# Wider MoE units: three units of 512 tokens in place of four of 384, in a gated-linear-attention and MoE kernel

## The chip, the core and the metric

The kernel runs as one program on one core of a Trainium2 chip. The engines named below are TensorE (PE, with its weight loads PEld), VectorE (DVE), ScalarE (ACT), GpSimd (POOL) and the engine that issues most DMAs (SP). The time of a run is the device time in microseconds (us); of several runs the median counts. A profile is one execution, recorded instruction by instruction; its span goes from the first to the last instruction.

## What is computed

The inputs are q, k, v and gate logits f for 4 sequences, 8 heads, 768 tokens and 48 features a head. The first half is a gated linear recurrence, whose output (4 sequences of 768 tokens, 8 x 48 = 384 features) is the input x of the second:

```
f = 1/(1+exp(-f_logit))
state = f[t] * state + outer(k[t], v[t]);   y[t] = q[t] @ state          # each head, t = 0..767
h = max(x @ w_in, 0)                                                     # 384 -> 1024 features
conv_out[t] = conv_w[0]*h[t-1] + conv_w[1]*h[t] + conv_w[2]*h[t+1]       # zero outside a sequence
out = (h * sigmoid(conv_out)) @ w_out                                    # 1024 -> 384
```

## The kernel before

**Chunks.** Attention works on chunks of 128 tokens: 24 chunks in all, 6 in a sequence. For each chunk n the order knows steps with a letter: F, L, M, V load f, k, q and v; x and p take exponentials and logarithms on ACT; G sums the logits; K and Q scale k and q (`scaled_q`, line 324: on POOL from chunk 5 on); k transposes k on PE (`ptk`, line 330); a computes the scores (`pa`, lines 345 and 351) and masks them on DVE; s adds to the state (`pk` on PE, lines 371 and 376, an addition on DVE, a product on POOL, line 386); y computes the output (`py`, line 398) in two halves, from the masked scores and from the state and the scaled q. The chunk's output goes, as a rounded part and a remainder, into the tile xT of its MoE unit.

**MoE units.** The 3072 tokens are cut into eight units of 384 tokens, two to a sequence. Unit u has for each of eight groups f of 128 features a step `m{u}.{f}` (`hidden`): nine matmuls into one PSUM tile `ph` (three slices of the 384 inputs, each as high x high, high x low and low x high part, line 454), the ReLU on ACT into h_b (line 457), the middle tap of the convolution on ACT (line 462) and the outer taps on DVE (lines 464 and 466). For each pair of groups there are `h{u}.{fp}` (`carried`: the last two columns of the unit before, or zeros, into h_b, ACT, line 435) and `j{u}.{fp}` (`gated`: tanh on ACT, line 473, and the product with h on DVE, line 475).

**Results.** `r{b}.{m}` (`result`) makes the output of one chunk: the gated values are split into a rounded part gh (ACT, line 493) and a remainder gl (DVE, line 495), 24 matmuls of 384 columns go into a PSUM tile `po` (line 507), ACT copies it out (line 512) and a DMA writes it. The tokens of one result can lie in two units, since a unit's last token waits for its right neighbour.

**Buffers.** The gated values of a unit are one tile of eight groups x 385 columns, of which there are two; the raw weights are staged in the same two buffers at the start. ph, po and some attention tiles share three PSUM buffers.

**The order.** Nothing is scheduled by the compiler. Every step is a generator; the table ORDER is a list of step names, and each mention runs its step on to its next `yield`. So the table alone sets the order in which the instructions of all steps stand on each engine; each engine works in that order and waits where an operand or a buffer is not ready. PE gets matmuls of several ph, po and attention steps in turn.

Of the kernel before, what the change touches and what calls it, by code (L numbers as in the profile page):

```python
# [9 lines left out]
F32 = mybir.dt.float32  # L10
# [7 lines left out]
P = 128  # L18
# [11 lines left out]
x5 V2 M3 K3 x4 y1 H1.0 J0.1 k2 a2 k2 a2 h0.2 x5 I1.1 O3 s1 y1 s1 F6 p3 J2.1 s1 J2.1 J2.1 H2.0 y1 Q3 J0.1 G4 J2.1 J1.1 G5  # L30
L5 H2.0 M5 s2 s2 y2 L6 p4 J0.1 p4 y2 J0.1 y2 J1.1 y2 Q4 J0.1 a3 h0.0 O0 x6 k3 J1.1 J1.1 V3 h0.6 m0.1 x6 F11 P3 H0.1 F8
s2 P3 H2.1 m0.3 m0.3 k3 t3 P3 K4 a3 J1.1 G6 m0.3 t4 m0.1 m0.1 y3 m0.1 P3 J1.1 y3 P3 m0.3 P0 p5 h0.4 s3 a4 y3 V6 P3 P0 p5
x8 s3 x8 V4 O5 K5 H0.1 F9 m0.0 O2 a4 m0.0 k4 m0.2 m0.0 P5 Q5 P5 m0.1 k4 m0.2 M6 m0.7 S3 m0.0 m0.1 H1.1 P0 P0 p6 p6 y3 P0
s3 S3 m0.4 F10 H2.1 m0.2 m0.0 a5 s4 y4 x9 m0.2 y4 P0 P2 H1.1 O4 P2 Q6 y4 G8 O6 a5 L8 m0.7 m0.5 M8 P5 m0.2 P5 s4 m0.7 t6
m0.7 L7 x9 s4 m0.1 V5 O1 m0.4 K6 y4 m0.3 m0.2 P5 m0.5 m0.4 m0.0 P2 t5 m0.6 m0.3 m0.0 P2 p7 m0.4 m0.5 V7 m0.6 K7 k6 m0.6
m0.5 m0.2 y5 m0.3 P5 y5 k6 p7 t7 y5 p8 m0.5 a6 k7 y5 m1.1 m0.6 a6 m1.0 M7 G9 M9 m0.4 S0 m1.3 m0.5 j0.0 m0.4 k7 m1.1 m1.1
P1 j0.2 S5 P2 m1.0 m1.0 p8 S0 F12 Q7 j0.0 a7 h1.0 L9 m1.1 s6 K8 S5 L10 s6 m0.7 Q8 m1.0 a7 y6 k8 P1 P1 m1.2 m0.5 m0.7
m1.3 k8 j0.2 P1 V9 m1.5 m0.6 h1.2 m1.2 m1.2 m0.4 p9 m1.5 m1.3 s7 P2 K9 P4 s7 P1 P4 j0.4 a8 y6 y6 m1.2 P4 P4 S2 m1.3 P1
F13 k9 p9 y7 k9 y7 m1.2 V8 m0.6 m1.4 j0.4 s7 m1.5 a8 m1.7 y7 m1.4 y7 m1.3 m1.4 F14 y8 m1.1 V11 m0.6 m0.7 y8 S1 x12 m1.3
a9 M10 t8 h1.4 L11 m1.5 S2 m1.2 Q9 P4 m1.4 G10 P4 O7 m1.5 P6 P6 a9 s8 j0.6 m1.4 j0.6 y8 S4 y8 h1.6 P6 m1.7 P7 m1.7 m1.2  # L40
s8 P7 m1.6 s8 m1.7 m1.6 M12 m1.6 m1.3 m2.3 p10 m2.3 p10 m2.2 a9 m2.3 m1.6 r0.0 m2.5 m2.2 m1.4 j1.2 L12 K10 r0.1 j1.2
m2.5 m2.2 P6 P6 S1 m2.5 k10 y9 k10 m2.3 m1.5 Q10 S4 a10 s9 m1.7 y9 M13 a10 m2.4 P6 h2.2 P7 P7 S6 m2.2 P7 m2.4 M11 r0.0
t9 r0.0 m1.5 m1.4 S6 j1.4 P7 j1.4 S7 m2.4 S7 m2.5 r0.0 r0.1 m1.1 m1.0 r0.0 y9 r0.0 r0.0 m1.6 r0.1 G11 m1.1 p11 m1.6 r0.1
# [684 lines left out]
```

## Time and profile before

| what | us |
|---|---|
| median of 3 runs | 305.09 |
| lowest and highest of them | 304.69, 307.47 |
| time of the profiled execution | 305.0 |
| its span | 303.3 |
| busy: PE / DVE / ACT / POOL | 294.2 / 251.3 / 220.5 / 85.3 |

The profiled execution took 0.1 us less than the median; 1.7 us of its time lie outside its span. Busy time of PE counts each matmul to its modelled end, and matmuls overlap: the next starts before the last has ended. So what one matmul costs is read from the distance of starts, not from its length.

### The profile page before, as it was taken

What the parts mean: (1) busy time and instruction counts of PE and PEld (TensorE: products, weight loads), DVE (VectorE), ACT (ScalarE), POOL (GpSimd) and SP (SyncE); (2) the same over time, 40 slices, a digit from 0 to 9 for tenths busy, and PEclk for the clock granted to TensorE, in tenths of its full rate; (3) what the DMA queues carried; (4) which work ended last, traced back from release to release, by engine and by line L of the source; (5) the groups of instructions that cost most, each with busy time, mean ns of one, the idle gap of its engine ahead of it and who ended that gap; (6) DMA issues with size and microseconds to landing.
All of it is one profiled execution on the core that took longest, in us unless ns stands there. A gap on an engine that the chain in (4) does not pass through costs nothing.

```text
span 303.3 us, 8894 instructions
## 1 busy us (share of the span) xinstructions
PE 294.2 (97%) x3747; PEld 273.5 (90%) x3747; DVE 251.3 (83%) x380; ACT 220.5 (73%) x422; POOL 85.3 (28%) x107
## 2 busy tenths in 40 slices
PE   7799989999999999999999999999999999999994
PEld 5678878988999999999998999999999999999994
DVE  4999999999999999977999999946893976479520
ACT  4999979989967996767976995665756544676521
POOL 5475894344503140300323410230305010000000
PEclk9999999999999999999999999999999999999999
DMA  7999951194025411627315130602012000000211
GB/s 230 396 385 391 403 191 39 56 333 135 2 72 161 101 59 61 220 72 224 102 37 166 64 124 2 195 2 84 3 30 89 2 28 26 28 1 2 79 54 55
DMA packets 19374, 35.67 MB, mean 118 GB/s; under 512 B 2156, under 2 KB 9092, under 8 KB 19332
## 3 DMA queue, kind: packets, MB, share of 16 engines
q1 hardware_dynamic: 19044, 34.69, 33.8%
q8 instruction: 30, 0.49, 0.7%
q10 hardware_dynamic: 288, 0.39, 0.4%
q14 instruction: 12, 0.10, 0.1%
HBM read 30.35 MB, written 4.72 MB: 116 GB/s over the span
## 4 chain that ended last, share of the span: by engine, by line
PE 75%; DVE 7%; POOL 3%; issue 1%; ACT 1%; POOLq 0%
PE po L507 31%; PE ph L454 28%; PE py L398 8%; PE pa L351 3%; PE ptk L330 2%; DVE g L466 2%; PE pk L376 2%; DVE g L464 2%; DVE g L475 1%; POOL st L386 1%; PE pa L345 1%; DVE am L358 1%; PE pk L371 1%; POOL q L324 1%; DVE gl L495 1%
## 5 line engine op out<-in xcount | busy, mean ns | idle before, releaser
L454 PE MATMUL ph<-xT,wih 128*128 128x384 f32 x384 | 99.6, 340 | 0.0
L454 PEld LDWEIGHTS ph<-xT,wih 128*128 128x128 f32 x384 | 68.3, 188 | 1.0 <-issue 0.2
L507 PE MATMUL po<-woh,gh 128*128 128x384 f32 x192 | 64.7, 337 | 0.0
L454 PE MATMUL ph<-xT,wil 128*128 128x384 f32 x192 | 64.3, 335 | 0.0
L507 PE MATMUL po<-wol,gh 128*128 128x384 f32 x192 | 64.2, 334 | 0.0
L507 PE MATMUL po<-woh,gl 128*128 128x384 f32 x192 | 64.2, 334 | 0.0
L464 DVE SCALAR_TENSOR_TENSOR g<-hb,cw,g 128x384 f32<-128x384 f32 (+1 forms) x64 | 42.2, 667 | 13.0 <-ACT g L462 12.9
L466 DVE SCALAR_TENSOR_TENSOR g<-hb,cw,g 128x384 f32<-128x384 f32 (+1 forms) x64 | 40.5, 649 | 0.7
L457 ACT ACTIVATE hb<-ph 128x384 f32<-128x384 f32 x64 | 30.7, 487 | 11.4 <-PE ph L454 10.8
L495 DVE TENSOR_TENSOR gl<-g,gh 128x1024 fp32r<-128x1024 f32 (+4 forms) x34 | 30.4, 908 | 9.6 <-ACT gh L493 9.6
L462 ACT ACTIVATE g<-hb,cw 128x384 f32<-128x384 f32 (+1 forms) x64 | 38.0, 614 | 0.3
L507 PEld LDWEIGHTS po<-woh,gh 128*128 128x128 f32 x192 | 36.0, 188 | 0.5 <-issue 0.2
L324 POOL TENSOR_TENSOR q<-q,fd 128x512 f32<-128x512 f32 x19 | 26.9, 1419 | 33.0 <-ACT fd L307 24.3
L507 PEld LDWEIGHTS po<-wol,gh 128*128 128x128 f32 x192 | 36.0, 188 | 0.0
L507 PEld LDWEIGHTS po<-woh,gl 128*128 128x128 f32 x192 | 36.0, 188 | 0.0
L454 PEld LDWEIGHTS ph<-xT,wil 128*128 128x128 f32 x192 | 36.0, 188 | 0.0
L493 ACT CAST gh<-g 128x1024 fp32r<-128x1024 f32 (+4 forms) x34 | 26.4, 800 | 12.7 <-PE po L507 8.8
L386 POOL TENSOR_TENSOR st<-st,ft_all 128x256 f32<-128x256 f32 x16 | 20.8, 1301 | 51.7 <-DVE st L384 51.7
L475 DVE SCALAR_TENSOR_TENSOR g<-g,hb 128x768 f32<-128x768 f32 (+1 forms) x32 | 30.1, 952 | 3.7 <-ACT g L473 3.7
L512 ACT COPY ob<-po 128x384 f32<-128x384 f32 x24 | 11.3, 474 | 29.7 <-PE po L507 27.1
L473 ACT ACTIVATE g<-g 128x768 f32<-128x768 f32 (+1 forms) x32 | 26.7, 846 | 3.9 <-DVE g L466 3.8
L312 POOL COPY ft_all<-fd 128x4 f32<-128x4 f32 x24 | 12.7, 537 | 56.5 <-ACT fd L307 56.5
(92 smaller groups left out, 453.9 us busy)
## 6 DMA issues: line engine op xcount, KB each, us to landing
k<-in_k_dram SPq DMA_DIRECT2D x24, 256.0 KB, 4.4
q<-in_q_dram SPq DMA_DIRECT2D x24, 256.0 KB, 4.3
v<-in_v_dram SPq DMA_DIRECT2D x24, 224.0 KB, 4.3
fb<-in_f_logit_dram SPq DMA_DIRECT2D x18, 256.0 KB, 4.3
out_dram<-ob SPq DMA_DIRECT2D x22, 192.0 KB, 1.9
wis<-in_moe_w_in_dram SPq DMA_DIRECT2D x6, 512.0 KB, 6.0
wos<-in_moe_w_out_dram SPq DMA_DIRECT2D x8, 384.0 KB, 5.6
fb<-in_f_logit_dram SPq DMA_DIRECT2D x6, 200.0 KB, 4.9
```

Of the source, the lines that this page charges most:

```text
L324: (nc.vector if n < QV else nc.gpsimd).tensor_tensor(raw["q", n], raw["q", n], fds[n][1], ALU.mult)
L398: nc.tensor.matmul(py[G * p:G * p + G, t, :], lhs, rhs, start=start, stop=stop)
L454: nc.tensor.matmul(ph, w, xts[b, hf][:, t, xl, :], start=(k == 0), stop=(k == 3 * KT - 1))
L457: nc.scalar.activation(hb[:, 2:HS + 2], ph, AF.Relu, scale=0.5)
L462: nc.scalar.activation(cv, hb[:, 1:n + 1], AF.Copy, scale=cw[:, 1, f:f + 1])
L464: nc.vector.scalar_tensor_tensor(cv, hb[:, 2:n + 2], cw[:, 2, f:f + 1], cv, ALU.mult, ALU.add)
L466: nc.vector.scalar_tensor_tensor(cv, hb[:, 0:n], cw[:, 0, f:f + 1], cv, ALU.mult, ALU.add)
L473: nc.scalar.activation(cv, cv, AF.Tanh)
L475: nc.vector.scalar_tensor_tensor(cv, cv, 1.0, h_b[:, fp:fp + 2, 1:n + 1], ALU.add, ALU.mult)
L493: nc.scalar.copy(hi, g[:, f:f + k])
L495: nc.vector.tensor_tensor(lo, g[:, f:f + k], hi.bitcast(F32), ALU.subtract)
L507: nc.tensor.matmul(po, g[:, f, :], w, start=(i == 0), stop=(i == 3 * NF - 1))
```

## The change

Units get lengths of their own: 384, 384, 512, 512, 512, 384, 384. Units 2, 3 and 4 hold tokens 768 to 2303 (sequences 1 and 2); unit 3 holds the last 256 tokens of sequence 1 and the first 256 of sequence 2. In unit 3 the ReLU writes two halves with a gap of one column between them, and that column is set to zero by a memset on POOL; likewise the column behind a sequence's end (units 1, 4 and 6, and before in one memset at the start). This makes 16 memsets of two columns in the program's order, four for each of these units. The gated values lie in one buffer of 16 slots, one for each group of features, and group f of unit u uses slot (8u + f) mod 16; the raw weights are staged in the same buffer. A unit of 512 needs four chunks of attention before its first matmul. ORDER differs from its third line on.

```
+    UL = (384, 384, 512, 512, 512, 384, 384)
+    UB = [sum(UL[:u]) for u in range(len(UL) + 1)]
+    GS = 16
+    KF = (B - 1, NC - UL[-1] // P - 1)
-    h_b = const.tile([P, NF, HS + 4], F32, name="hb")
-    nc.gpsimd.memset(h_b[:, :, HS + 2:], 0.0)
+    h_b = const.tile([P, NF, UM + 4], F32, name="hb")
+    g_b = const.tile([P, GS, UM + 2], F32, name="gb")
...
+        def slot(u, f):
+            return (NF * u + f) % GS
         def carried(u, fp):
-            nc.scalar.copy(h_b[:, fp:fp + 2, 0:2], h_b[:, fp:fp + 2, HS:HS + 2] if u % 2 else
-                           going[:, :2, 0:1].broadcast_to([P, 2, 2]))
+            z = going[:, :2, 0:1]
+            e = 2 + width(u - 1) - last(u - 1) if u else 0
+            nc.scalar.copy(h_b[:, fp:fp + 2, 0:2], h_b[:, fp:fp + 2, e - 2:e] if UB[u] % S else z.broadcast_to([P, 2, 2]))
+            if inner(u):
+                nc.gpsimd.memset(h_b[:, fp:fp + 2, 2 + inner(u):3 + inner(u)], 0.0)
+            if last(u):
+                nc.gpsimd.memset(h_b[:, fp:fp + 2, 1 + width(u):2 + width(u)], 0.0)
             yield
         def hidden(u, f):
-            ph = ps.tile([P, HS], F32, tag="mm", name=f"ph{u}_{f}", bufs=MB)
+            L, n, s = UL[u], width(u), inner(u)
+            ph = ps.tile([P, L], F32, tag="mm", name=f"ph{u}_{f}", bufs=MB)
...
+            if s:
+                ho = hb[:, 2:2 + L + 2].rearrange("p (a c) -> p a c", a=2)[:, :, :s]
+                nc.scalar.activation(ho, ph.rearrange("p (a c) -> p a c", a=2), AF.Relu, scale=0.5)
+            else:
+                nc.scalar.activation(hb[:, 2:L + 2], ph, AF.Relu, scale=0.5)
-            cv = gts[u][:, f, :n]
+            cv = g_b[:, slot(u, f), :n]
...
 ORDER (a line of each):
-x5 V2 M3 K3 x4 y1 H1.0 J0.1 k2 a2 k2 a2 h0.2 x5 I1.1 O3 s1 y1 s1 F6 p3 J2.1 s1 J2.1 J2.1 H2.0 y1 Q3 J0.1 G4 J2.1 J1.1 G5
+x5 V2 M3 K3 x4 y1 H1.0 J0.1 k2 a2 k2 a2 h0.2 x5 I1.1 O3 s1 y1 s1 F6 p3 J2.1 s1 J2.1 J2.1 H2.0 y1 V3 G4 G5 s2 Q3 y2 F8 y2
```

What that does to the engines is seen at three places.

PE, the start of unit 2. Before, its first groups (ph_3, ph_2, ph_5) follow each other ahead of any result:

```order
L454 MATMUL ph_6_1248<-xT_1_630,wil_1_706 128x384
L454 MATMUL ph_3_1263<-xT_0_1069,wih 128x384 x2
L454 MATMUL ph_3_1263<-xT_0_1069,wil_0_271 128x384
L454 MATMUL ph_3_1263<-xT_0_1069,wih 128x384 x2
L454 MATMUL ph_3_1263<-xT_0_1069,wil_0_388 128x384
L454 MATMUL ph_2_1274<-xT_0_1069,wih 128x384 x2
```

Now the same unit starts between matmuls of the first two results, and each of its matmuls has 512 columns:

```order
L519 MATMUL po_0_1351<-woh,gl_0_1237 128x384
L465 MATMUL ph_3_1415<-xT_1056,wih 128x512 x2
L465 MATMUL ph_3_1415<-xT_1056,wil_0_269 128x512
L519 MATMUL po_1_1379<-woh,gh_1_1327 128x384
L519 MATMUL po_1_1379<-wol_1270,gh_1_1327 128x384
L519 MATMUL po_1_1379<-woh,gl_1_1328 128x384
```

The results of chunks 0 and 1 were moved ahead of unit 2, which now waits for chunk 9 in place of chunk 8. Over the whole program PE has 72 ph matmuls fewer (216 of 512 columns in place of 288 of 384) and the same po and attention matmuls.

POOL, early in the program: mswo is the staging of w_out, q_... the scaling of a chunk's q, st the product of the state. Before:

```order
L179 TENSOR_SCALAR mswo_607<-wos_409 128x384
L181 TENSOR_SCALAR mswo_607<-mswo_607 128x384
L179 TENSOR_SCALAR mswo_670<-wos_642 128x384
L324 TENSOR_TENSOR q_458<-q_458,fd_610 128x512
L181 TENSOR_SCALAR mswo_670<-mswo_670 128x384
L386 TENSOR_TENSOR st_77<-st_77,ft_all 128x256
L179 TENSOR_SCALAR mswo_762<-wos_409 128x384
L181 TENSOR_SCALAR mswo_762<-mswo_762 128x384
L324 TENSOR_TENSOR q_680<-q_680,fd_693 128x512
```

and now:

```order
L178 TENSOR_SCALAR mswo_591<-gb 128x384
L180 TENSOR_SCALAR mswo_591<-mswo_591 128x384
L310 COPY ft_all<-fd_551 128x4
L322 TENSOR_TENSOR q_499<-q_499,fd_551 128x512
L384 TENSOR_TENSOR st_77<-st_77,ft_all 128x256
L178 TENSOR_SCALAR mswo_753<-wos 128x384
L178 TENSOR_SCALAR mswo_756<-gb 128x384
L180 TENSOR_SCALAR mswo_756<-mswo_756 128x384
L180 TENSOR_SCALAR mswo_753<-mswo_753 128x384
L384 TENSOR_TENSOR st_78<-st_78,ft_all 128x256
L322 TENSOR_TENSOR q_492<-q_492,fd_666 128x512
```

The state product for chunk 4 (st_77) has one staging pair less ahead of it, and chunk 6's scaled q (q_680, now q_492) one pair and a state product more.

PE, the end of the last unit. Before, all its ph matmuls stand ahead of seven results of 24 matmuls each:

```order
L454 MATMUL ph_5_3759<-xT_1_3415,wil_1_706 128x384
L454 MATMUL ph_2_3755<-xT_1_3415,wih 128x384 x2
L454 MATMUL ph_2_3755<-xT_1_3415,wil_0_456 128x384
L507 MATMUL po_4_3798<-woh,gh_4_3623 128x384
L507 MATMUL po_4_3798<-wol_945,gh_4_3623 128x384
```

Now result 2.4 (po_4) stands in two halves between them, and six results follow the last one:

```order
L519 MATMUL po_4_3661<-wol_1392,gh_4_3544 128x384
L519 MATMUL po_4_3661<-woh,gl_4_3545 128x384
L465 MATMUL ph_5_3675<-xT_3233,wih 128x384 x2
L465 MATMUL ph_5_3675<-xT_3233,wil_1_693 128x384
L465 MATMUL ph_5_3675<-xT_3233,wih 128x384 x2
L465 MATMUL ph_5_3675<-xT_3233,wil_1_607 128x384
L519 MATMUL po_0_3707<-woh,gh_0_3697 128x384
```

The third of the results that follow, 3.2, needs the last unit's gated values; it now stands 48 po matmuls behind the unit's last matmul, before 72.

## Rows read from the trace of the kernel before

**Rows 1.** The page, part 1: busy us, share of the span, instructions of each engine.

```profile
PE 294.2 (97%) x3747; PEld 273.5 (90%) x3747; DVE 251.3 (83%) x380; ACT 220.5 (73%) x422; POOL 85.3 (28%) x107
```

**Rows 2.** Busy us by stretch: PE, PEld, DVE, ACT, POOL, granted clock, DMA share, GB/s.

```profile
0.00:44.00 44.00, 39.01 (x623) 32.26 (x623) 39.68 (x63) 37.68 (x78) 29.92 (x46) 1.00 0.93 344
44.00:138.00 94.00, 93.97 (x1276) 87.32 (x1264) 89.43 (x138) 77.85 (x149) 29.85 (x38) 1.00 0.36 112
138.00:166.00 28.00, 28.00 (x492) 25.81 (x482) 27.07 (x38) 22.95 (x40) 7.54 (x7) 1.00 0.40 123
166.00:258.00 92.00, 91.88 (x1159) 87.05 (x1150) 72.55 (x107) 59.73 (x112) 17.99 (x17) 1.00 0.17 54
258.00:303.30 45.30, 41.39 (x239) 41.07 (x237) 22.57 (x37) 22.26 (x46) 0.00 (x0) 1.00 0.10 36
```

**Rows 3.** The chain that ended last, in order of time: start us, us, what.

```profile
104.10 8.32 PE po L507 x48
...
257.79 12.48 PE ph L454 x72
270.27 29.14 PE po L507 x168
...
299.43 0.48 ACT ob L512
```

**Rows 4.** Waits of PE: releaser, us in total, times, longest us.

```profile
PE pl L292 <- ACT fb L271: 1.7, 2, 1.1
...
PE py L398 <- POOL st L386: 1.1, 1, 1.1
```

**Rows 5.** Timeline of PE, two stretches: start us, us from first start to last end.

```profile
20.00 0.66 PE L330 MATMUL ptk<-ident,k 128*128 128x128 f32 x4
20.58 1.16 PE L345 MATMUL pa<-q,k 48*128 48x128 f32 x16
...
48.94 0.60 PE L330 MATMUL ptk<-ident,k 128*128 128x128 f32 x4
49.29 0.60 PE L454 MATMUL ph<-xT,wih 128*128 128x384 f32 x2
49.72 0.34 PE L454 MATMUL ph<-xT,wil 128*128 128x384 f32 x1
49.99 1.08 PE L398 MATMUL py<-am,v 128*32 128x128 f32 x32
```

**Rows 6.** Groups by form, DVE and ACT: busy us, mean ns | idle before, releaser.

```profile
L457 ACT ACTIVATE hb<-ph 128x384 f32<-128x384 f32 x64 | 30.7, 487 | 11.4 <-PE ph L454 10.8 <-DVE g L475 0.4
...
L464 DVE SCALAR_TENSOR_TENSOR g<-hb,cw,g 128x384 f32<-128x384 f32 x32 | 20.6, 651 | 1.5 <-ACT g L462 1.4
...
L462 ACT ACTIVATE g<-hb,cw 128x384 f32<-128x384 f32 x32 | 19.3, 614 | 0.1
...
L475 DVE SCALAR_TENSOR_TENSOR g<-g,hb 128x768 f32<-128x768 f32 x16 | 15.2, 951 | 3.7 <-ACT g L473 3.7
...
L473 ACT ACTIVATE g<-g 128x768 f32<-128x768 f32 x16 | 13.4, 845 | 1.0 <-DVE g L466 0.9
...
L495 DVE TENSOR_TENSOR gl<-g,gh 128x254 fp32r<-128x254 f32 x4 | 1.4, 416 | 0.0
L493 ACT CAST gh<-g 128x254 fp32r<-128x254 f32 x4 | 1.3, 402 | 1.6 <-PE po L507 1.6
```

**Rows 7.** Timeline of POOL around 36 us: start us, us.

```profile
35.55 0.88 POOL L179 TENSOR_SCALAR mswo<-wos 128x384 f32<-128x384 f32 x1
36.40 1.74 POOL L324 TENSOR_TENSOR q<-q,fd 128x512 f32<-128x512 f32 x1
38.23 0.89 POOL L181 TENSOR_SCALAR mswo<-mswo 128x384 f32<-128x384 f32 x1
39.08 4.27 POOL L386 TENSOR_TENSOR st<-st,ft_all 128x256 f32<-128x256 f32 x1
```

**Rows 8.** Single lines of POOL: duration ns min/median/max, first and last start us.

```profile
L386 POOL TENSOR_TENSOR st<-st,ft_all x16: 610/925/4271, 23.8 to 247.7; 128x256 f32<-128x256 f32 x16
...
L339 POOL MEMSET am<- x2: 526/534/542, 67.5 to 79.3; 128x512 f32 x2
```

More of the change, by code (lines that the diff above doesn't have):

```diff
@@ L34 @@
[L34 to L43, printed above, removed]
@@ L233, in split_w_out @@
     def split_w_out(f):
-        slot = dict(tag="wi", bufs=NWI) if f == 0 and WHOLE_OUT else dict(tag="wo", bufs=NF)
-        yield from split(("o", f), woh[:, f], f"wol{f}", **slot)
+        yield from split(("o", f), woh[:, f], f"wol{f}", tag="wo", bufs=NF)
     def load_cw():
@@ L387, in state, with unit_of, new_x @@
         yield
-    xts = {(0, 0): wk.tile([P, KT, 2, HS], F32R, tag="xT", name="xT0_0", bufs=3)}
+    def unit_of(t):
+        return max(u for u in range(len(UL)) if UB[u] <= t)
+    def new_x(u):
+        return wk.tile([P, KT, 2, UL[u]], F32R, tag="xT", name=f"xT{u}", bufs=3)
+    xts = {0: new_x(0)}
     def values(n):
@@ L469, in gated @@
         def gated(u, fp):
-            n = HS + u % 2
-            cv = gts[u][:, fp:fp + 2, :n]
+            n = width(u)
+            cv = g_b[:, slot(u, fp):slot(u, fp) + 2, :n]
             has_logs.clear()
@@ L500, in result @@
             for f in range(NF):
[L501 to L508 removed]
+                hi, lo = woh[:, f], wlo["o", f]
+                for g, w in ((gh, hi), (gh, lo), (gl, hi)):
+                    nc.tensor.matmul(po, g[:, f, :], w, start=(i == 0), stop=(i == 3 * NF - 1))
+                    i += 1
                 if f % 2:
@@ L517, in unit @@
         def unit(u):
-            b, hf = u // 2, u % 2
             todo = {}
@@ L524, in unit, with ready @@
                 todo[f"j{u}.{fp}"] = gated(u, fp)
-            for m in range(CPH - 1) if hf == 0 else range(CPH - 1, NC):
-                todo[f"r{b}.{m}"] = result(b, m)
-            return todo
-        return unit
+            return todo
+        def ready(u):
+            return [n for n in range(B * NC)
+                    if unit_of((n + 1) * P - 1) + (any((n + 1) * P == UB[w + 1] and not last(w) for w in range(len(UL)))) == u]
+        return unit, result, ready
     n_ft = B * NC * NP
@@ L569, in gla_moe_kernel @@
         todo[f"O{f}"], todo[f"P{f}"], todo[f"S{f}"] = load_w_out(f), single_w_out(f), split_w_out(f)
-    unit = moe(xts, wk, ps, WHOLE, WHOLE_OUT)
-    for u in range(2 * B):
+    unit, result, _ = moe(xts, wk, ps)
+    for u in range(len(UL)):
         todo.update(unit(u))
+    for n, (b, c) in enumerate(steps):
+        todo[f"r{b}.{c}"] = result(b, c)
     for e in ORDER.split():
```

233 lines of the change are left out of this document (112 added, 121 removed).

## The prediction, written before the changed kernel ran

> **What bounds the kernel now.** I read the busy shares first. PE is busy 294.2 of 303.3 us and DVE, the next, 251.3 [rows 1]. The table by stretches says where that holds: from 44 to 258 us PE has no idle time worth naming, and its clock is granted in full, the 2.4 GHz level, in all five stretches [rows 2]. Between 138 and 166 us DVE is busy 27.1 of 28.0 us beside it, so there two engines are near their limit; later DVE falls back (72.6 of 92 us) and has slack. The chain of waits ends in the same picture: 12.5 us of ph matmuls and 29.1 us of po matmuls in one piece, then a copy of 0.5 us and the last DMA [rows 3]. PE's own waits are few: 1.7 us at the start for the first gate and 1.1 us for one state product of POOL [rows 4]. So the end is set by the length of PE's stream, and by whatever new bubble the other engines put into it. An engine that gets faster off that stream gives nothing by itself.
>
> **The change, part by part.**
>
> *Fewer, wider ph matmuls.* A ph or po matmul of 384 columns costs PE 0.1733 us: 48 of them take 8.32 us, 168 take 29.14, and 72 ph ones 12.48 [rows 3]. The change removes 4 units x 8 groups x 9 = 288 of these (49.9 us) and adds 3 x 8 x 9 = 216 of 512 columns. No row has that width, so I bound it. If the whole price goes by columns, it is 0.1733 x 512/384 = 0.2311, and 216 cost 49.9 us: nothing gained. At the granted 2.4 GHz 384 columns at one a cycle take 0.160 us; the other 0.0133 may belong to a matmul rather than to its columns. Then the new price is 0.1733 + 128/2400 us = 0.2267, 216 cost 49.0 us, and the gain is 0.96 us. The lowest end is 512 columns with nothing around them, 0.2133: 46.1 us, a gain of 3.8. I take 0.2267, which changes least against the row, and keep 0 and -3.8 for the range.
>
> Behind that stands a rule. The Trainium skill, TensorE: Matmul & The Clock Gate, section Back-to-back issue gap, gives N/2.4 + 2.5 ns for the isolated gap at full clock: 162.5 ns for 384 columns and 215.8 for 512. The trace disagrees at 384 by 10.8 ns; by the page at both widths the change would gain 0.2 us, and by the row at 384 with the page at 512 3.3 us.
>
> *Junctions on PE.* All po and attention matmuls stay, but their neighbours change, and a junction has a price. A ph or po matmul ahead of a narrow one lasts 0.27 us to the next start (49.72 to 49.99), so 0.10 more than among its like [rows 5]. By the order there were 18 of these and are now 16: -0.2 us. Four transposes cost 0.35 us when ph follows (48.94 to 49.29) and 0.58 when scores follow (20.00 to 20.58) [rows 5]. That second kind stood once and now stands four times: +0.7. The rest of the pairs comes out slightly lower. I take +0.4, ends 0 and +0.7.
>
> *DVE.* A tap of the convolution costs 0.651 us for 384 columns [rows 6]. From 254 to 768 columns DVE goes from 416 to 951 ns, 1.04 ns a column [rows 6], though with different operations at the ends. Two taps each lose 32 and gain 24: 2 x (8 x 0.651 - 24 x 128 x 0.00104) = 4.0 us less; the products with h go from 16 to 12: 0.6 us. So about 4.6 us of DVE go. They lie beside PE's stream, which has no idle time there to give back [rows 2], so I book nothing.
>
> *ACT.* In the same way, at 0.86 ns a column (402 ns at 254, 845 at 768): ReLU 1.3, middle tap 2.3, tanh 0.7 us, and four carries [rows 6]; 4.2 us or more go. Nothing is booked here either: ACT waits for PE's ph rather than the reverse (10.8 us of idle ahead of the ReLU [rows 6]).
>
> *The ring and the units over two sequences.* Sixteen slots are two units of eight groups, as the two tiles were, so no buffer is lost; a slot comes free by itself, which can only loosen a wait. The split in unit 3 keeps the number of results that are cut in two at four.
>
> *Sixteen memsets on POOL.* A memset of 512 columns took 0.53 us both times [rows 8], so two columns cost no more: under 8.5 us in all, and POOL is idle for 218 [rows 1]. What counts is what queues behind one that waits. In unit 3 a memset waits for unit 2's gated product on DVE, and the scaling of q for chunk 15 stands behind it. The ACT carry of the same step waits for the same product, so the planner's place is no later than what the unit needs anyway: 0.
>
> *POOL early.* The state product that PE waits for now (39.08, done at 43.35 [rows 7]) has one staging pair less ahead, 0.88 + 0.89 us [rows 7]: the wait of 1.1 us may go. That pair and another product stand instead ahead of chunk 6's q, so the lateness can come back there. I book 0, ends -1.1 and +1.1.
>
> *The end.* Result 3.2 comes 48 po matmuls (8.3 us) behind the last ph, before 72 (12.5 us). In that time ACT has the last ReLU and tap (0.49 + 0.61), four tanh (3.4) and four quarter splits (1.6), 6.1 us; DVE has three taps, four splits and three products, 2.0 + 1.7 + 2.9 = 6.6 us [rows 6]. Both fit, with some 2 us to spare. SP's loads stay the same in number; the DMA share is 0.40 or less after 44 us [rows 2].
>
> **Sum**: the profiled execution's 305.0 (span 303.3 and 1.7 around it) - 0.96 + 0.4 = 304.4 us. The median of the runs shown is 0.1 above that execution, so against it this is -0.2%.
>
> **The rivals.**
>
> *The extra of 0.0133 us vanishes at 512 columns* (something else than columns holds the 384-wide matmul back, a weight load for instance). Then 305.0 - 3.8 + 0.4 = 301.6. Against it: four transposes with weights of the same 128 x 128 take 0.35 us in all [rows 5], so a load fits into some 0.1 us and cannot make 0.173.
>
> The formula of the Trainium skill, TensorE: Matmul & The Clock Gate, section Back-to-back issue gap, belongs to this rival: with its 215.8 ns at 512 and the row's 0.1733 us at 384 the time would be 302.1 us.
>
> *POOL's two-input work is held up at a place where PE has no slack*: slower. The state product takes 0.61 us at best and took 4.27 once [rows 7, 8], in the stretch where DVE is busy 39.7 of 44 us and POOL 29.9 [rows 2]. That one stretch gave today's 1.1 us wait. In the rewritten order other products meet PE's need at other distances; if one is stretched by 3.66 us where PE arrives just on time, the time is 304.4 + 3.7 = 308.1. It decides from the point where a product has under 3.7 us to spare. For it: the order was rewritten from the third line on, and this stretching depends on what DVE happens to do. Against: DVE has 4.6 us less to do, and POOL is idle 72% of the time [rows 1].
>
> The Trainium skill, SBUF: State Buffer, section SBUF: two separate sides, states the mechanism: a DVE operation with two SBUF inputs and a POOL operation that reads SBUF hold their shared ports exclusively, and the other is blocked. By that rule the new memsets, which read nothing, are not held up, and the trace agrees: 526 and 542 ns [rows 8].
>
> *Nothing is gained*: the matmul goes by columns (0), junctions are at +0.7, and small waits come to as much as 1 us, at unit 2's later start (chunk 9 in place of 8) or at result 3.2: 305.0 + 0.7 + 0.5 = 306.2, ends 305.4 and 307.
>
> **How the numbers follow.** Forecast 0.64 (own range 303.4 to 305.4), vanishing extra 0.08, held-up POOL 0.14, nothing gained 0.14. The range, 302.6 to 307.6, takes in the forecast, nothing gained, a wait of POOL that goes (-1.1) or a partly held-up product; it leaves out the first rival and most of the second. One per cent, about what a measurement of this kernel can tell from no change, is 3.05 us: below 302.0 lies the first rival alone, 0.07; above 308.1 lies most of the second (one held-up product gives just that, two give more) and the far end of nothing gained, 0.13; the rest, 0.80, is within.
>
> **What would show it.** In the new profile: starts of 512-wide ph matmuls 0.227 us apart (0.231 or 0.213 decide the ends); PE without idle time from 44 us to some 4 us before the end; DVE near 247 and ACT near 216 us busy; junctions of transposes and scores at 0.58; POOL's state products ending before PE asks. The forecast is wrong if PE shows a wait of over 1 us past 50 us, or if its last matmul ends before 296 us (299.4 now [rows 3]).

## The result and the profile after

The changed kernel took 306.93 us (median of 20 runs, 305.30 to 310.21) where the kernel before took 304.96 on the same chip: 1.006 times as long, interval 1.0035 to 1.0085. A second measurement gave 306.90 against 304.16, 1.0088 (1.0058 to 1.0119). So it is slower by 0.6 to 0.9%, inside the 1% that the prediction called no change and inside its range, but on the other side of its 304.4, and outside the forecast's own range of 303.4 to 305.4. Some executions of any of these kernels run some per cent longer at a lower granted clock; the ratios and their 95% intervals leave them out, so a ratio is not exactly the quotient of the two medians.

Two executions of it were profiled, of 306.12 and 307.06 us. The first page line and the PE waits of the first, columns as in [rows 1] and [rows 4]:

```profile
PE 294.1 (97%) x3675; PEld 263.8 (87%) x3675; DVE 250.1 (82%) x360; ACT 218.0 (72%) x398; POOL 84.9 (28%) x122
```

```profile
PE pl L290 <- ACT fb L269: 2.5, 2, 1.6
PE pa L343 <- DVE q L322: 1.6, 2, 0.9
...
PE ph L465 <- DVE xT L428: 0.3, 1, 0.3
```

The waits of PE in the second execution:

```profile
PE pl L290 <- ACT fb L269: 2.2, 2, 1.6
PE pw L170 <- POOL st L131: 1.2, 1, 1.2
PE py L402 <- DVE xT L428: 1.2, 2, 0.9
PE pa L343 <- DVE q L322: 0.9, 2, 0.5
PE ptk L328 <- DVE st L384: 0.7, 1, 0.7
PE ph L465 <- DVE xT L428: 0.3, 1, 0.3
```

PE's wait for POOL's state product, the 1.1 us of [rows 4], is gone from both. In its place PE waits for DVE, at three kinds of steps and at other places in each execution. Where, the stretches of the second execution tell (columns as in [rows 2]):

```profile
0.00:44.00 44.00, 39.12 (x625) 32.39 (x626) 39.53 (x64) 38.29 (x81) 26.82 (x47) 1.00 0.93 335
44.00:138.00 94.00, 91.78 (x1227) 80.93 (x1226) 91.09 (x132) 76.59 (x137) 33.10 (x42) 1.00 0.37 118
138.00:166.00 28.00, 28.00 (x454) 23.40 (x452) 23.52 (x31) 23.34 (x37) 7.19 (x11) 1.00 0.39 125
166.00:258.00 92.00, 92.00 (x1139) 83.98 (x1124) 70.97 (x96) 56.34 (x98) 18.46 (x23) 1.00 0.15 49
258.00:305.30 47.30, 43.45 (x251) 43.12 (x249) 26.37 (x42) 23.25 (x47) 0.00 (x0) 1.00 0.11 39
```

From 138 us to the end of its stream PE is never idle, as the prediction had it. Between 44 and 138 us it now lacks 2.2 us (0.03 in [rows 2]); in the first execution it lacks less there, 0.65 us, and 0.8 us more before 44:

```profile
0.00:44.00 44.00, 38.22 (x622) 31.68 (x623) 39.06 (x63) 38.03 (x80) 25.21 (x46) 1.00 0.93 336
44.00:138.00 94.00, 93.35 (x1234) 82.37 (x1233) 91.08 (x135) 77.93 (x140) 35.18 (x43) 1.00 0.37 120
```

DVE has become free where it hurt nobody, 23.5 of 28 us between 138 and 166 (27.1 in [rows 2]), and is as full as ever in the start.

For the comparisons below I add up PE's stream block by block; a block is a group of matmuls of one kind in a row (four transposes, sixteen scores, a run of ph). Take the time from the first matmul of a block to the first of the next (for ph and po less 0.1733 or 0.2267 us a matmul). What it has beyond the shortest such time for the same pair of kinds in any of these profiles is called **idle** here, and one such piece a **bubble**; the rest is **work**. The level of both hangs on which pairs are taken as alike; what is read from them is the difference between profiles, and pairing in another way moves a difference by up to some 0.3 us. For the kernel before: work 288.30 us, idle 3.68 before 20 us, 3.38 from 20 to 80, 2.64 after; its last matmul ends at 299.39. For the two changed profiles: work 287.77, idle 4.06 and 3.72, then 4.59 and 5.57, then 2.68 and 2.98; the last matmul ends at 300.52 and 301.45. So work fell by 0.53 us, and the idle time of the first 80 us, where both kernels still do units 0 and 1 of 384 tokens, rose by 1.6 and 2.2 us. Of the 1.6, 0.4 us lie before 20 us, where PE's steps are still the same in both orders, in the wait for the first gates. The loss lies where no wide unit has yet begun. The medians lie 2.0 and 2.7 us apart, the profiled ends 1.1 and 2.1: 0.7 to 0.8 us of the difference is in no profile.

### The profile page after: what moved, and what is told of

The parts are those of the page before. It is cut to its first block, busy times and chain, and to the rows that moved or that the text cites. A ratio compares the mean times of both kernels' runs of the same rounds, so it can differ in the third digit from the quotient of the medians.

```text
span 304.4 us, 8734 instructions
## 1 busy us (share of the span) xinstructions
PE 294.1 (97%) x3675; PEld 263.8 (87%) x3675; DVE 250.1 (82%) x360; ACT 218.0 (72%) x398; POOL 84.9 (28%) x122
## 4 chain that ended last, share of the span: by engine, by line
PE 72%; POOL 2%; DVE 1%; issue 1%; ACT 1%; POOLq 0%
PE po L519 33%; PE ph L465 25%; PE py L402 7%; PE pa L349 3%; PE pk L374 2%; PE ptk L328 2%; POOL mswo L178 1%; POOL mswo L180 1%; POOL q L322 0%; DVE am L353 0%; DVE fb L295 0%; ACT mswo L182 0%; ACT gb L476 0%; DVE gb L478 0%; DVE wo L188 0%
## 5 line engine op out<-in xcount | busy, mean ns | idle before, releaser
L465 PE MATMUL ph<-xT,wih 128*128 128x384 f32 (+1 forms) x336 | 95.7, 365 | 0.3 <-DVE xT L428 0.3
L465 PE MATMUL ph<-xT,wil 128*128 128x384 f32 (+1 forms) x168 | 60.4, 360 | 0.0
L511 DVE TENSOR_TENSOR gl<-gb,gh 128x1024 fp32r<-128x1024 f32 (+4 forms) x34 | 30.9, 919 | 15.1 <-ACT gh L509 14.9
L478 DVE SCALAR_TENSOR_TENSOR gb<-hb,cw,gb 128x384 f32<-128x384 f32 (+3 forms) x56 | 37.9, 696 | 2.6 <-ACT gb L476 2.5
L509 ACT CAST gh<-gb 128x1024 fp32r<-128x1024 f32 (+4 forms) x34 | 26.7, 801 | 17.9 <-PE po L519 14.3
L480 DVE SCALAR_TENSOR_TENSOR gb<-hb,cw,gb 128x384 f32<-128x384 f32 (+3 forms) x56 | 38.6, 709 | 0.4
L489 DVE SCALAR_TENSOR_TENSOR gb<-gb,hb 128x768 f32<-128x768 f32 (+3 forms) x28 | 31.9, 1150 | 7.3 <-ACT gb L487 7.3
L476 ACT ACTIVATE gb<-hb,cw 128x384 f32<-128x384 f32 (+3 forms) x56 | 36.3, 660 | 0.3
L473 ACT ACTIVATE hb<-ph 128x384 f32<-128x384 f32 (+1 forms) x48 | 24.8, 523 | 10.1 <-PE ph L465 9.3
L487 ACT ACTIVATE gb<-gb 128x768 f32<-128x768 f32 (+3 forms) x28 | 25.6, 935 | 4.9 <-DVE gb L480 4.7
L402 PE MATMUL py<-am,v 128*32 128x128 f32 x768 | 25.9, 275 | 0.3 <-DVE xT L428 0.3
```

Source lines behind the costliest of these rows:

```text
L402: nc.tensor.matmul(py[G * p:G * p + G, t, :], lhs, rhs, start=start, stop=stop)
L465: nc.tensor.matmul(ph, w, xts[u][:, t, xl, :], start=(k == 0), stop=(k == 3 * KT - 1))
L473: nc.scalar.activation(hb[:, 2:L + 2], ph, AF.Relu, scale=0.5)
L476: nc.scalar.activation(cv, hb[:, 1:n + 1], AF.Copy, scale=cw[:, 1, f:f + 1])
L478: nc.vector.scalar_tensor_tensor(cv, hb[:, 2:n + 2], cw[:, 2, f:f + 1], cv, ALU.mult, ALU.add)
L480: nc.vector.scalar_tensor_tensor(cv, hb[:, 0:n], cw[:, 0, f:f + 1], cv, ALU.mult, ALU.add)
```

## The experiments

All ratios are to the kernel before, run beside it on the same chip. The expectations call the explanations by letters: S, the rewritten order of the first 80 us costs the time; W, the wide products save nothing; R, the ring and its memsets cost it; J, the junctions of the new order do, over the whole span; then, within S: V, VectorE has no pause and delivers single steps late; Q, GpSimd or a transfer is late and VectorE only passes it on. A **seam** is the place in a table at which the old sequence of steps gives way to the new one, or the reverse.

**The storage alone, and the changed kernel again.** The first takes the changed code with eight units of 384 and the old order; the second has no edit.

```diff
-    UL = (384, 384, 512, 512, 512, 384, 384)
+    UL = (384,) * 8
-ORDER = (of the changed kernel)
+ORDER = (of the kernel before)
```

> The changed code (ring of 16 slots, memsets in the carried step, raw weights staged in the ring) with eight units of 384 and the old order throughout: the storage alone. Theories S and W, and the prediction on record (ring and memsets at nothing): 0.998 to 1.002 times the kernel before. Rival R (the ring costs the time): 1.004 to 1.008.

> The changed kernel once more, as it is, for a second profile and a ratio on the same chip as the kernels beside it. Its first profiled execution was 1.1 us longer than that of the kernel before, the median of its runs 2.0 us. Theory S (the order of the first 80 us, rewritten, leaves TensorE idle for about 1.3 us more) and theory W (the 512-wide hidden products save nothing, since they run above their median of 0.227 us beside narrow work): both expect 1.004 to 1.008 times the kernel before, and bubbles in the same places as in the first profile (2.1 us near 5 us, 0.9 us near 34 us, 0.6 us near 52 us). If it was only scatter: 1.000 to 1.003, and bubbles in other places.

Measured: the storage alone 304.32 us, 1.0001 (0.9979 to 1.0024): ring, memsets and the raw weights in the ring cost nothing, rival R falls. The changed kernel again 1.0088, just above what was expected, with bubbles of 0.5 us near 34 (0.9 in the first profile) and 0.7 near 52 as in the first, and new ones of 1.0 us near 59 and 72. The loss is not that of one scattered run, but the places of the bubbles shift.

**The old start in the changed kernel.** Four kernels take the first 460, 358, 388 and 410 steps of the old order and then the remaining steps in the new one; the fourth also puts steps that come late at this seam up to 34 places earlier. As a rule, in place of the table's rows:

```diff
-for e in ORDER.split():
+head = OLD_ORDER.split()[:388]      # 460, 358, 410
+rest = (ORDER.split(), the first occurrence of each step of head left out)
+for e in head + rest:
```

> The changed kernel with the first 460 steps of the order (all up to the first step of unit 2, near 80 us) in the sequence of the kernel before; the remaining steps keep their new sequence. Theory S (the rewritten start costs 1.3 us of idle TensorE): the 0.9 us bubble near 34 us and the 0.6 us bubble near 52 us are gone, idle in the first 80 us back near 6.0 us, the time 1.3 us or more below the changed kernel, 0.999 to 1.002 times the kernel before. Theory W (wide products): no gain, still 1.004 to 1.008 times the kernel before. Rival R (the ring of 16 slots and its memsets on GpSimd hold something up): also 1.004 to 1.008.

Measured: 308.73 us, 1.015 (1.0109 to 1.0191), against both theories. The trace gives the reason. Up to 74 us its start was clean; then PE stood still, since the old head has no step of chunk 10 yet and the new rest puts these behind other work. PE's timeline there (start us, us):

```profile
75.67 0.34 PE L466 MATMUL ph<-xT,wil 128*128 128x384 f32 x1
77.81 0.84 PE L329 MATMUL ptk<-ident,k 128*128 128x128 f32 x4 [1.80 <-issue]
79.39 0.90 PE L350 MATMUL pa<-q,k 48*64 48x128 f32 x32 [0.74 <-POOL q L323]
```

A seam has a price of its own; this run tells the theories apart only by what stands ahead of it: from 20 to 73 us it has no bubble above 0.4 us. The next seams were put where fewer steps differ.

> The changed kernel with the first 358 steps of the order (to about 55 us) as the kernel before has them, then the new sequence. It leaves the seam where few steps differ; in the run whose seam was at 460 steps the start was clean until 74 us and the seam itself then cost 4 us, because the steps of chunk 10 came late. Counted over tokens 768 to 2303 the hidden products take 50.56 us of TensorE in the changed kernel and 51.81 in the one before, so the wide units do gain 1.25 us. Theory S (the new start loses it): idle of TensorE between 20 and 60 us 1 us below the changed kernel (which has 2.9 to 3.6), the seam at most 0.5 us, the time 303.5 to 305 where the kernel before has 304.2, ratio 0.997 to 1.003. Rival J (the loss is in the junctions of the new order everywhere): 1.005 or more, and the idle time spread over the whole span.

> As the run before it, with the first 388 steps (to about 60 us). Theory S: the start is clean for longer, but a8, p9 and V8 come later than in either order; 0.997 to 1.005, with any idle time of TensorE between 60 and 75 us. Rival J: 1.005 or more without a bubble there.

> The changed kernel with the first 410 steps of the old order (to about 65 us) and the new order from there, the steps that come late at this seam (loads of q of chunk 10 and k of chunk 11, scaling of q of chunk 9, the sums of chunk 10, a load of raw weights) put 10 to 30 steps earlier. With the seam at 388 steps it was 1.001 with 3.4 us of idle TensorE between 20 and 80 us. Theory S, carried on: 0.997 to 1.000, idle there near 2.7 us (as in the ring with old units and old order), the end 0.3 us below that kernel's by the wide units and their junctions. If the seam costs again: 1.001 to 1.006.

Measured: 358 steps 305.51 us, 1.0040 (1.0026 to 1.0054), outside its range; 388 steps 304.91, 1.0008 (0.9982 to 1.0034), within it; 410 steps 304.97, 1.0027 (1.0003 to 1.0050), a miss for theory S carried on. The longer old head of 388 steps gives back the whole loss, the 358 about half. In the 388-step kernel idle from 20 to 80 us is 3.65 us, work 287.69, and the last matmul ends at 298.95, 0.44 ahead of the kernel before. None of them has a ratio below 1: the gain of the wide units is there in the profile and not resolved in the ratios.

**The new start with old units.** The reverse: the ring with eight units of 384 and slots of 514, the first 360 steps new, the rest old. (A first try, with 488 new steps and slots of 386, measured 1.026, over its 1.003 to 1.006; a bubble of 4.8 us behind its seam is in that. In it unit 1, by its code, writes over raw output weights before they are used, so part of these weights are wrong. Only its first 80 us are read here, below.)

> The ring with eight units of 384 (its slots 514 wide, as in the changed kernel), the first 360 steps in the new sequence, the remaining ones in the old one. The same with the old sequence throughout measured 1.000. Theory S: bubbles near 34 and 52 us (and after them), idle 1 to 2 us more in the first 80 us, 1.003 to 1.007 times the kernel before. Rival J: 1.000 to 1.002.

Measured: 306.44 us, 1.0063 (1.0041 to 1.0084). With no wide unit in the program, this kernel costs what the changed kernel costs. It has a seam of its own at step 360, and its only profile is its slowest execution (310.36 us), so by itself it does not show that the new start takes the 0.6%. The first try has the new sequence and units of 384 up to some 83 us, ahead of its seam: there its idle from 20 to 80 us is some 6.2 us (3.38 in the kernel before), with bubbles of 1.2 us near 35, 0.7 near 52 and 1.1 near 73. And the 388-step kernel has all the wide units and loses nothing. Together they speak for theory S against W and J: the start loses the time, not the wide units.

**Single late steps.** What is late in the start? First, near 34 us, VectorE in the first changed profile, and then in the kernel with less VectorE work, told of below (start us, us, idle before and releaser):

```profile
33.57 0.69 DVE L315 TENSOR_TENSOR k<-k,fi 128x512 f32<-128x512 f32 x1 [0.52 <-DMA k<-in_k_dram]
34.18 0.69 DVE L188 CUSTOM_DVE_ANT_0 wi<-gb,mswi 128x1024 uint16<-128x1024 uint16 x1
34.78 0.69 DVE L322 TENSOR_TENSOR q<-q,fd 128x512 f32<-128x512 f32 x1
```

```profile
34.00 0.69 DVE L317 TENSOR_TENSOR k<-k,fi 128x512 f32<-128x512 f32 x1 [2.35 <-DMA k<-in_k_dram]
```

VectorE waits for the load of k of chunk 5, and the scaling of q of chunk 4, for which PE waits, stands two steps behind it. (In the second changed profile VectorE does not wait there, and PE's bubble of 0.5 us stands all the same.) In the new order that load is some 20 steps later and that scaling some 45. Two kernels put them back, the first one also moves the copy and the difference of y of chunk 5 ahead of a masking:

```diff
-G4 G5 s2 Q3 y2 ... x6 L5 J0.1 P3 ... P0 P0 Q4 O2 s3
+G4 G5 L5 s2 Q3 y2 ... Q4 x6 J0.1 P3 ... P0 P0 O2 s3
-t7 a6 L8 m0.6 x9 S0 P5 y5 S0 k7 m0.6 y5     (first kernel only)
+t7 y5 L8 m0.6 x9 y5 a6 S0 P5 S0 k7 m0.6
```

> The changed kernel with four steps moved: the load of k of chunk 5 some 20 steps earlier (the old place), the scaling of q of chunk 4 on VectorE some 45 steps earlier, the copy and the difference of y of chunk 5 ahead of the masking of chunk 7. Theory S, in its narrow form (single late steps make the bubbles): the bubble near 34 us (0.94 and 0.54 us in two profiles) and the one near 52 us (0.6 us) go, 1.0 to 1.5 us less, ratio 1.002 to 1.004 where the changed kernel has 1.006 to 1.009. If VectorE as a whole is the limit in this stretch, the bubbles move to other places and the ratio stays above 1.005.

> The changed kernel with that load and that scaling alone at their old places. The bubble near 34 us (0.94 and 0.54 us) goes. If the weight preparation simply runs 0.5 to 1 us later everywhere else, the bubbles at 50 to 73 us grow by as much (with one more step moved they had grown from 2.7 to 4.6 us): 1.005 to 1.011. If the load was an independent cost: 1.003 to 1.006.

Measured: 307.94 us, 1.0108 (1.0072 to 1.0143), and 306.59, 1.0052 (1.0017 to 1.0088). The bubble near 34 us is gone in both, but idle from 20 to 80 us is 6.44 and 5.04 us, no less than in the changed kernel (4.59 and 5.57); bubbles of 1.1 us stand near 72 in both. The first ratio is as expected if VectorE as a whole is the limit; the second lies in both of its ranges and decides nothing. A step that is moved forward pushes another back, which points to an engine with nothing to spare.

**Which engine.** Edits, in this order: the mantissa step of the raw weights (VectorE) cut to a quarter of the columns, in the changed kernel twice and in the kernel before; the sign step (GpSimd) cut in the same way (VectorE then reads that quarter four times, so its work stays); and eight subtractions moved from VectorE to GpSimd, with the new and with the old start. Where a step is cut, the kernel leaves out the preparation of part of the weights.

```diff
-        nc.vector.scalar_tensor_tensor(m, m, 3, s, ...)
+        h = n // 4
+        nc.vector.scalar_tensor_tensor(m[:, :h], m[:, :h], 3, s[:, :h], ...)
```

```diff
-        nc.gpsimd.tensor_scalar(sf, mf, 0.0, 1.0, ALU.mult, ALU.mult)
+        nc.gpsimd.tensor_scalar(sf[:, :h], mf[:, :h], 0.0, 1.0, ALU.mult, ALU.mult)
```

```diff
-ON_POOL = ""
+ON_POOL = "o"
```

> The changed kernel with a lighter VectorE in the start: the step that sets the mantissa of the raw weights (14 of them, ten between 20 and 80 us at 0.65 to 0.83 us each) works on a quarter of the columns only, so the weights in the other columns are wrong and so is what is computed with them; nothing else is left out. About 4 us less VectorE work between 20 and 80 us. Theory V (in the new start VectorE, busy without a pause, delivers single steps late, and TensorE waits for them): idle of TensorE between 20 and 80 us falls from 4.3 to 5.6 us to under 3.4, the time to 0.998 to 1.003 times the kernel before, where the changed kernel has 1.006 to 1.009. Rival Q (the late steps wait for GpSimd or for a transfer, and VectorE only passes it on): 1.005 or more, and the bubbles near 52, 59 and 72 us stay.

> The changed kernel with the mantissa step on a quarter of the columns, as measured once at 1.002 (the weights in the other columns are wrong): a second ratio beside the relief of GpSimd, and a profile. Theory V: again 0.999 to 1.004, idle of TensorE between 20 and 80 us 1.5 to 3 us where the changed kernel has 4.3 and 5.6. Rival Q: 1.005 or more.

> The kernel before with the same step cut to a quarter of the columns (the same part of the weights is wrong). Its TensorE is idle 3.4 us between 20 and 80 us, of which 1.3 us wait for GpSimd's product of the state. Theory V: little to win, 0.995 to 1.000 times the kernel before, less than the changed kernel wins by it. If both win the same, the changed start is no more bound by VectorE than the old one.

> The changed kernel with a lighter GpSimd in the start: its second step on each raw weight (the one that takes the sign) works on a quarter of the columns and VectorE reads that quarter four times, so the signs of the other weights are wrong. VectorE has as much to do as before. Theory V (VectorE is what is late): 1.005 or more, idle of TensorE between 20 and 80 us still 4 us or more. Rival Q (GpSimd is late and VectorE passes it on): 1.003 or less, idle there under 3.4 us.

> The changed kernel with the eight subtractions that give the low part of the output weights on GpSimd in place of VectorE (0.55 us each on VectorE, between 50 and 85 us). Theory V: the bubbles near 59, 62 and 72 us shrink, 0.5 to 1 us less than the changed kernel, 1.002 to 1.006. Rival Q: no gain or a loss, 1.006 to 1.012, since GpSimd has more to do and its subtraction reads two inputs and holds VectorE up while it runs.

> The changed kernel with the first 388 steps in the old sequence (1.001) and the same eight subtractions on GpSimd. A candidate that may beat both: theory V 0.996 to 1.000; if the moved work holds GpSimd's own products up, 1.001 to 1.005.

Measured: less VectorE work 304.68 us, 1.0020 (0.9993 to 1.0046), and again 304.37, 0.9996 (0.9961 to 1.0031); the kernel before with it 303.43, 0.9983 (0.9953 to 1.0012); less GpSimd work 304.92, 1.0018 (0.9982 to 1.0053); work moved to GpSimd 309.41, 1.0155 (1.0086 to 1.0223), and with the old start 310.30, 1.0190 (1.0109 to 1.0271). Relief of either engine gives back most or all of the loss, so neither theory V nor Q holds alone: V missed the relief of GpSimd, Q that of VectorE, and both missed how much the moved work costs.

Idle from 40 to 80 us is 1.21 and 1.07 us with VectorE relieved and 1.20 with GpSimd relieved, against 2.68 and 3.88 in the changed kernel. From 20 to 80 us, the stretch that theory V named, it is some 2.9 us with GpSimd relieved, but 5.5 and 6.7 with VectorE relieved, a miss: the two profiled executions are longer than the medians (306.63 and 308.66 us), VectorE itself waits 2.35 and 3.0 us in them near 34 us for the load of k of chunk 5, and PE waits 2.0 and 2.3 us behind it. The kernel before falls as well, from 2.46 to 1.00 us between 40 and 80: it too is near this limit, and whether the changed start is nearer to it these intervals do not tell.

How the two engines hold each other up can be read near 59 us of the second changed profile. PE, then VectorE, then GpSimd:

```profile
59.18 0.34 PE L465 MATMUL ph<-xT,wil 128*128 128x384 f32 x1
60.27 0.44 PE L328 MATMUL ptk<-ident,k 128*128 128x128 f32 x2 [0.75 <-DVE st L384]
```

```profile
58.10 1.78 DVE L315 TENSOR_TENSOR k<-k,fi 128x512 f32<-128x512 f32 x1
59.80 0.41 DVE L384 TENSOR_TENSOR st<-pk,ft_all 128x256 f32<-128x256 f32 x1
```

```profile
57.27 2.05 POOL L322 TENSOR_TENSOR q<-q,fd 128x512 f32<-128x512 f32 x1
```

The product on VectorE takes 0.69 us elsewhere (33.57 above) and 1.78 here, while a product of two inputs runs on GpSimd, which itself takes 2.05 us (1.30 us at 45.22 of this profile). The state that PE waits for stands behind it on VectorE and is 0.75 us late. The same is seen ahead of the bubble near 72 us of this profile (VectorE 1.69 us, 0.55 elsewhere; GpSimd; the step of PE that comes late):

```profile
67.67 1.69 DVE L186 SCALAR_TENSOR_TENSOR mswo<-mswo 128x384 int32<-128x384 int32 x1
67.66 1.28 POOL L322 TENSOR_TENSOR q<-q,fd 128x512 f32<-128x512 f32 x1
73.73 1.08 PE L402 MATMUL py<-am,v 128*32 128x128 f32 x32 [0.95 <-DVE xT L428]
```

In the kernel before such pairs stand too, without a wait of PE behind this one:

```profile
44.90 1.80 DVE L317 TENSOR_TENSOR k<-k,fi 128x512 f32<-128x512 f32 x1
44.54 1.61 POOL L324 TENSOR_TENSOR q<-q,fd 128x512 f32<-128x512 f32 x1
```

How much of this a start has can be added up. Take each VectorE operation that starts between 20 and 80 us and is more than 0.08 us longer than the median of the same operation over all profiles of this case: 210 operations in 19 profiles, and each of them overlaps an operation of GpSimd (of the others 64% do). What they have beyond the median comes to 3.1 us in the kernel before, 3.0 with the ring alone and 3.2 with 388 old steps; 4.3 and 6.0 in the changed kernel; 6.0 and 5.7 with single steps moved; 6.1 and 7.7 with the subtractions on GpSimd; 2.7 and 3.0 with VectorE relieved and 2.5 with GpSimd relieved. So one cause fits the relief by either engine and the loss by the moved work: in the new sequence the two engines hold each other up more. It goes along with the loss, with one exception (4.1 in the long profiled execution of the last kernel below). No run changes the overlap alone, so as the cause it is likely and not shown.

**Both mechanisms together.** The relief of VectorE and the earlier load and scaling in one kernel, edits as above.

> The changed kernel with the mantissa step on a quarter of the columns (the weights in the other columns are wrong), and the load of k of chunk 5 and the scaling of q of chunk 4 at their old places, some 20 and 45 steps earlier. If the late load near 34 us and the weight preparation from 45 to 80 us are the whole loss of the start: idle of TensorE between 20 and 80 us 1.5 to 2 us (1.5 in the kernel before with the same relief), no bubble over 0.4 us there, 0.995 to 0.999 times the kernel before. If something else in the new order holds TensorE up: 3 us idle or more, and 1.000 or more.

Measured: 304.33 us, 0.9997 (0.9974 to 1.0021), just outside the range. Its profiled execution, the slowest of ten at 307.37 us, has the bubble near 34 us gone and 1.16 us of idle from 40 to 80, but a bubble of 2.5 us inside the products near 25 us, so idle from 20 to 80 us is some 6.0 us, a miss. What PE waits for there the trace does not show; in four other long executions (306.90 to 314.27 us) it waits 0.6 to 2.1 us near 26 us for the load of v. Whether late loads are a part of the loss of the start by themselves no run tells, and that the load and the weight preparation are the whole of it is not shown.

PE, DVE and the other engines from 20 to 40 and from 40 to 80 us, columns as in [rows 2]: the kernel before, the changed one (second profile), the one with 388 old steps, and the one with GpSimd relieved.

```profile
20.00:40.00 20.00, 19.72 (x310) 17.57 (x304) 19.88 (x30) 19.19 (x44) 14.09 (x16) 1.00 1.03 392
40.00:80.00 40.00, 38.87 (x553) 34.70 (x550) 39.47 (x62) 36.46 (x72) 22.55 (x26) 1.00 0.38 123
```

```profile
20.00:40.00 20.00, 19.17 (x309) 16.71 (x302) 19.89 (x30) 18.95 (x42) 12.81 (x15) 1.00 0.95 348
40.00:80.00 40.00, 37.99 (x568) 33.05 (x564) 39.97 (x60) 33.26 (x68) 20.74 (x28) 1.00 0.43 140
```

```profile
20.00:40.00 20.00, 19.75 (x303) 17.57 (x304) 19.88 (x29) 19.30 (x44) 13.52 (x16) 1.00 1.04 389
40.00:80.00 40.00, 39.09 (x656) 33.96 (x652) 39.68 (x63) 35.52 (x71) 21.04 (x29) 1.00 0.37 117
```

```profile
20.00:40.00 20.00, 19.20 (x316) 16.48 (x314) 19.62 (x30) 18.53 (x41) 11.74 (x15) 1.00 0.98 352
40.00:80.00 40.00, 40.00 (x635) 35.13 (x634) 39.90 (x64) 36.07 (x76) 20.97 (x30) 1.00 0.44 143
```

From 20 to 80 us VectorE is busy 59.4 of 60 us before, and 59.4 and 59.9 in the two changed profiles. In all it has next to nothing to spare, so the sequence of its steps, and what stretches them, decide which of PE's needs comes late. In the changed kernel also less is loaded from 20 to 40 us (351 and 348 GB/s in place of 392).

## Why the prediction was wrong

**Wider ph matmuls, -0.96 us: right.** PE's timeline in the second changed profile, one run of ph directly after po (start us, us):

```profile
91.72 0.63 PE L465 MATMUL ph<-xT,wih 128*128 128x512 f32 x2
92.18 0.40 PE L465 MATMUL ph<-xT,wil 128*128 128x512 f32 x1
92.42 0.62 PE L465 MATMUL ph<-xT,wih 128*128 128x512 f32 x2
...
94.48 0.62 PE L465 MATMUL ph<-xT,wih 128*128 128x512 f32 x2
...
96.52 0.62 PE L465 MATMUL ph<-xT,wih 128*128 128x512 f32 x2
97.20 0.62 PE L465 MATMUL ph<-xT,wih 128*128 128x512 f32 x2
```

From 94.48 to 97.20 twelve starts lie 0.2267 us apart on average, the price taken. From 91.72 to 92.42 three take 0.70 us, 0.233 each: the first few after other work run slower. Over all ph of tokens 768 to 2303, bubbles and junctions included, the trace before has 51.81 us for 288 and both changed ones 50.56 for 216: -1.25. Neither 0.231 nor the 0.2133 of the first rival came, nor the 0.2158 that the formula of the Trainium skill gives at 512 columns (TensorE: Matmul & The Clock Gate, section Back-to-back issue gap).

**Junctions, +0.4: right in size.** The counts came as taken: wide matmuls ahead of narrow ones 18 and 16, transposes ahead of scores one and four. The three new ones of the second kind cost 0.53 us each, not 0.58, so +0.55 in place of +0.7. All work on PE fell by 0.53 us (288.30 to 287.77); -0.96 and +0.4 make -0.56. That they agree so closely is in part luck, since this difference too is good to some 0.3 us only.

**DVE -4.6 and ACT -4.2 us, booked at nothing: right there, wrong where they were used again.** VectorE's relief came from 138 to 166 us (27.1 to 23.5). The taps gave more than the 4.0 us taken (82.7 to 76.5 us over the span), the products with h rose by 1.8 us (30.1 to 31.9) instead of falling by 0.6; that the two together came near 4.6 is luck. Over the span VectorE's busy time is 250.1 and 251.5 us, not the 247 expected, in part since operations of the start were stretched by 1.2 and 3.0 us more; the rest stays open. ACT's is 218.0 and 217.8, not 216. The prediction also set it against the rival of held-up products: "Against: DVE has 4.6 us less to do". In the first 80 us it has not: 59.4 us busy of the 60 from 20 to 80 before, 59.4 and 59.9 after. The argument moved a saving from one stretch into another.

**POOL early, booked at 0 with ends of 1.1 us: this is the step that failed.** The wait for the state product went, as it allowed: in the first changed profile that product takes 0.62 us in place of 4.27 [rows 7].

```profile
38.91 0.62 POOL L384 TENSOR_TENSOR st<-st,ft_all 128x256 f32<-128x256 f32 x1
```

(Ahead of chunk 6's scaled q only one state product was added. The staging pair stood ahead of it before as well, on the other side of chunk 4's product.) But the rewritten start, from the third line of the table on, was priced by this one wait. It had to be priced by the stretch from 20 to 80 us as a whole, where [rows 2] shows DVE busy 39.7 of 44 us and then 89.4 of 94 beside POOL's weight preparation. There the new sequence cost 1.2 and 2.2 us of idle in the two profiles (4.59 and 5.57 against 3.38), and the kernel with the new start and old units lost 0.6%. The sign came from there. The prediction's own sign of being wrong, a wait of PE of over 1 us past 50 us, did not show: the longest in the view of waits is 0.95 us. The loss is made of pieces that are each below it; the other sign, PE without idle time from 44 us on, did fail.

**Ring, memsets, units over two sequences, the end: right at 0.** The ring alone measured 1.0001. After 80 us idle is 2.68 and 2.98 us, against 2.64.

**The sum.** -0.53 of work, +1.6 and +2.2 of idle in the first 80 us, 0.0 and +0.3 after it: +1.1 and +2.0 us, and the two profiled ends differ by 1.1 and 2.1 (300.52 and 301.45 against 299.39).

**The rivals.** The second, POOL's two-input product colliding with DVE, came nearest in its mechanism: 308.1 at 0.14. It is the one near 59 and 72 us, but in small pieces of PE's time of up to 1.0 us, and it is VectorE's step that is stretched and passes it on. The third (306.2) came nearest in size, by luck: its cause, columns at full price, junctions at the upper end and small waits at unit 2 or at the last result, did not come; the waits came ahead of both. The Trainium skill, SBUF: State Buffer, section SBUF: two separate sides, says that a two-input operation of VectorE and a reading one of GpSimd lock each other out of their shared ports; the rows near 59 us agree, 1.78 us in place of 0.69, with VectorE's operation ending 0.56 us after GpSimd's.

## What to carry to other kernels

Price a rewritten order stretch by stretch, and first where a second engine is busy without pause: there a step that moves forward moves another back, and "off the path" is no reason for 0. A saving on an engine counts only in the stretch in which it falls; from 138 us on it cannot pay for 50 us. And bubbles that move from one profile to the next while the total stays pointed here to a full engine and not to a late step: mending single steps gave nothing clear (1.0108, 1.0052), taking work from VectorE or GpSimd (0.9996 to 1.0020) or keeping the old sequence (1.0008) did. Where two engines hold each other up, add up how far the operations of one exceed their usual length: here that told the starts apart where busy shares did not (59.4 and 59.9 of 60 us).

## What the runs showed of the hardware that was not expected

A wait of PE of 2 us cost more than itself. In the profiled execution of the kernel with less VectorE work, 2 us above its median, PE waited 2.0 us near 34 us, and then (start us, us):

```profile
37.63 0.99 PE L467 MATMUL ph<-xT,wih 128*128 128x384 f32 x2
38.42 0.52 PE L467 MATMUL ph<-xT,wil 128*128 128x384 f32 x1
38.74 0.84 PE L467 MATMUL ph<-xT,wih 128*128 128x384 f32 x2
39.38 0.52 PE L467 MATMUL ph<-xT,wil 128*128 128x384 f32 x1
```

From 38.42 to 38.74 one matmul takes 0.32 us, not 0.173, at the 1.2 GHz level of the clock. The stretches around it (columns as in [rows 2]):

```profile
30.00:34.00 4.00, 3.94 (x81) 2.93 (x79) 1.65 (x3) 3.08 (x7) 0.56 (x2) 1.00 1.03 374
34.00:40.00 6.00, 4.05 (x27) 3.93 (x28) 6.00 (x10) 4.67 (x10) 4.18 (x5) 0.77 0.63 236
40.00:44.00 4.00, 4.00 (x59) 3.56 (x61) 2.73 (x6) 2.62 (x7) 2.32 (x4) 0.91 0.94 315
```

The granted clock is 0.77 of full from 34 to 40 us and 0.91 from 40 to 44; the nine ph matmuls that began at 37.63 are 1.5 us longer than the same at full clock. It is not a single case. Behind the wait of 2.3 us in the second profile with less VectorE work the granted clock is 0.92 from 34 to 40 us and 0.69 from 40 to 44, and behind the one near 25 us in the kernel with both edits:

```profile
28.00:34.00 6.00, 6.00 (x67) 5.38 (x68) 4.22 (x7) 4.53 (x11) 2.14 (x4) 0.72 0.75 253
```

The waits of 0.5 to 1.0 us in the changed kernel's two profiles left the clock at 1.00 from 20 to 80 us, and so did one of 1.3 us near 26 us in the kernel with 410 old steps.
